# The low halves of one chunk's normalized rows, computed on DVE instead of POOL (attention, Fourier mixing and a feed-forward layer on one core)

## Chip, cores and metric

One core of a Trainium2 chip runs the whole kernel in one launch. The metric is the device time of that launch in microseconds (us), the median of several runs. The names of the engines are those of the profile: PE multiplies matrices (PEld is its weight load), DVE, ACT and POOL work elementwise, SP issues the DMAs.

## What is computed

```python
# q, k, v: (8, 8, 576, 64), phi: (8, 8, 576, 32), w_ch1: (512, 2048), w_ch2: (2048, 512), all f32
a = softmax(phi, axis=2)
k_m, v_m = a^T k, a^T v                        # 32 memories per head
attn = softmax(q k_m^T / 8) v_m                # per head
x = attn of all heads side by side             # (8, 576, 512)
u = x + real(fft(fft(x, axis=1), axis=2))
un = (u - mean(u)) / sqrt(var(u) + 1e-6)       # per row of 512
out = u + max(un @ w_ch1, 0) @ w_ch2
```

## The kernel before

The 4608 rows of the feed-forward layer form 36 tiles of 128 rows, and two tiles are a chunk: 18 chunks, numbered from 0. `background()` makes the tiles of `u` batch by batch (pooling, memories, scores, mixing); the feed-forward layer of one chunk runs while the background makes a later one.

**Chunk 0** is multiplied in f32 straight from the freshly decoded weights. The weights come in as 64-bit words, in 8 pieces j = 0..7 of `w1` and of `w2`. For each j the loop prepares a piece of `w1` (`prepare_w1`), multiplies (`ffn1_direct`, L701, PSUM tiles `ph_j_f`), prepares a piece of `w2` (`stage_w2`), multiplies again (`ffn2_direct`, L718, accumulating in `po_0` and `po_1`) and splits the piece of `w1` into f16 halves for the later chunks (`split_w1`). Preparing a piece is `to_f32`: ACT takes the high words (L797), DVE shifts them (L799) and joins sign and exponent (L800), and then the low words are folded in. For most pieces DVE folds (L810). For `w2` pieces 0, 2, 4 and 6 (the list `LP`) DVE shifts the low words (L805) and **POOL** adds them (L808). So PE's multiplication with `w2` piece 4 waits for POOL's L808 of that piece.

**Chunks 1 to 17** are multiplied in f16 pairs, high and low half. `norm_chunk(c)` makes them: the rows are normalized into `un` (POOL takes the root, L667; DVE scales, L668), ACT rounds both tiles to f16 into `ud[:, 0]` (L687), POOL subtracts, `ud[:, 1] = un - ud[:, 0]` (L688, 128 x 1024 elements), and SP issues one transposing DMA of `ud` into `unring` (L241). PE reads `unring` in `ffn1` (L258). Chunk 1 is normalized inside chunk 0's loop, as soon as four tiles of `u` exist.

The order on each engine is set ahead of time by a scheduler that simulates the program; within an engine, and in SP's queue of DMAs, instructions run strictly in that order. In SP's queue chunk 1's transposing DMA stands ahead of the weight loads (L787) of `w2` piece 6 and of both piece 7's.

```python
nc.gpsimd.tensor_tensor(out=d, in0=lo, in1=d, op=ALU.add)       # L808, pieces 2_0, 2_2, 2_4, 2_6
```

Of the kernel before, what the change touches and what calls it, by code (L numbers as in the profile page):

```python
# [16 lines left out]
ALU = mybir.AluOpType  # L17
# [114 lines left out]
def kernel(  # L132
# [10 lines left out]
    nc = tc.nc  # L143
# [21 lines left out]
    un = const.tile([P, CH, DM], F32, name="un")  # L165
    ud = const.tile([P, 2, CH, DM], F16, name="ud")
# [71 lines left out]
    def transpose(dst, src, on_pe, key):  # L238

        if not on_pe:  # L240
            nc.sync.dma_start_transpose(out=dst, in_=src)  # L241
            return
        n = src.shape[1] // P
        for i0 in range(0, n, 8):
            m = min(8, n - i0)
            pt = psg.tile([P, 512], F32, tag="g", name=f"pt_{key}_{i0}")
            ptv = pt.bitcast(F16)[:, : m * P]
            for i in range(m):
                nc.tensor.transpose(ptv[:, i * P : (i + 1) * P], src[:, (i0 + i) * P : (i0 + i + 1) * P], ident)
            nc.scalar.copy(out=dst[:, i0 : i0 + m], in_=ptv.rearrange("p (a c) -> p a c", c=P))  # L250
# [402 lines left out]
    def norm_tile(i, u, un):  # L653
        mv = tiny("mv", 2, 2)
        if i < 2 * BN:
            st = tiny("st", 6, 2)
            nc.vector.bn_stats(out=st, in_=u)
            nc.vector.bn_aggr(out=mv, in_=st)
        else:
            st = tiny("st", 6, 2)  # L660
            nc.scalar.activation(un, u, AF.Copy, scale=-1.0 / DM, accum_out=st[:, 0:1])
            nc.scalar.activation(un, u, AF.Square, bias=st[:, 0:1], accum_out=st[:, 1:2])
            nc.vector.tensor_scalar(out=mv[:, 0:1], in0=st[:, 0:1], scalar1=-1.0, scalar2=None, op0=ALU.mult)
            nc.vector.tensor_scalar(out=mv[:, 1:2], in0=st[:, 1:2], scalar1=1.0 / DM, scalar2=None, op0=ALU.mult)
        rs = tiny("rs", 1, 2)
        nc.vector.tensor_scalar(out=rs, in0=mv[:, 1:2], scalar1=1e-6, scalar2=0.25, op0=ALU.add, op1=ALU.mult)  # L666
        nc.gpsimd.tensor_tensor(out=rs, in0=rs, in1=half, op=ALU.pow)  # L667
        marks[f"un{i}"] = nc.vector.tensor_scalar(  # L668
            out=un, in0=u, scalar1=mv[:, 0:1], scalar2=rs, op0=ALU.subtract, op1=ALU.mult
        )  # L670

    def norm_chunk(c):

        unT = unring[:, c % 2]
        unT0 = unT.rearrange("p l t k c -> p (l t k c)").bitcast(F32)
        unT0 = unT0.rearrange("p (k t c) -> p k t c", k=NK, t=CH)
        for i in range(CH):
            idx = CH * c + i
            norm_tile(idx, us[idx], un[:, i])
            if c == 0:  # L680
                pt = psg.tile([P, 512], F32, tag="g", name=f"pt_unT_{i}")
                for k in range(NK):
                    nc.tensor.transpose(pt[:, k * P : (k + 1) * P], un[:, i, k * P : (k + 1) * P], identf)
                marks["uh0"] = nc.scalar.copy(out=unT0[:, :, i], in_=pt.rearrange("p (k c) -> p k c", k=NK))  # L684
        if c == 0:
            return unT0
        marks[f"uh{c}"] = nc.scalar.copy(out=ud[:, 0], in_=un)  # L687
        marks[f"ul{c}"] = nc.gpsimd.tensor_tensor(out=ud[:, 1], in0=un, in1=ud[:, 0], op=ALU.subtract)  # L688
        transpose(
            unT.rearrange("p l t k c -> p (l t k) c"), ud.rearrange("p l t c -> p (l t c)"), False, f"unT_{c}"  # L690
        )
        return unT
# [181 lines left out]
    marks = {}  # L874
# [100 lines left out]
    while made < 2:  # L975
        made, room = next(bg)
    unTs = {0: norm_chunk(0)}
    hs = {c: [] for c in range(n_chunks)}
    po = [ps2.tile([P, 512], F32, tag="o", name=f"po_0_{t}") for t in range(CH)]
    for j in range(NW):  # L980
        if j not in parts_w1:
            load_weights(j)
        after(GATE1[j], prepare_w1, j)
        ffn1_direct(j)
        after(GATE2[j], stage_w2, j)
        ffn2_direct(j, po)
        split_w1(j)
        advance(0, steps=STEPS)
        if made >= 2 * CH and 1 not in unTs:
            unTs[1] = norm_chunk(1)  # L990
# [15 lines left out]
    run_ffn1(NW + 4)  # L1006
    advance(CH, CH * 3)
    unTs[2] = norm_chunk(2)
    for n in range(NW, n_steps):
        c, j = divmod(n, NW)  # L1010
# [75 lines left out]
```

## Time and profile before

| | |
|---|---|
| time, median of 3 runs (lowest, highest) | 1002.51 us (1002.23, 1004.06) |
| span of the profiled execution | 1006.9 us |
| PE busy in it | 959.2 us (95%) |
| DVE, ACT, POOL busy | 567.1, 454.0, 233.0 us |
| L688 on POOL: 17 instructions | 45.1 us in all |

The span is the time from the first to the last instruction of one profiled execution. No other time of that execution is given. It is 4.4 us (0.4%) above the median of the unprofiled runs, so a sum worked out in the span is carried over to the median as a difference. Rows give times in us from the start of the span.

### The profile page before, as it was taken

The page shows a single profiled execution, that of the slowest core. Times are in us where ns is not written, and L with a number is a line of the kernel's source. Part 1 is how long each engine was busy: PE and PEld are TensorE (multiplying, and loading weights), DVE is VectorE, ACT ScalarE, POOL GpSimd, SP SyncE. Part 2 cuts the span into 40 slices and gives each one's busy share as a digit, 9 for nine tenths or more (in the row PEclk, how much of TensorE's full clock was granted, in tenths as well). Part 3 has the DMA queues.
Part 4 walks back from the last instruction along what each step waited for, and adds up shares of the span by engine and source line. Part 5 has one row for each costly group of instructions (what it writes and reads, how often), then busy time and mean ns, then how long its engine had stood idle before and what let it go on. Part 6 is the DMA issues. An engine that isn't in the chain of part 4 may idle for free.

```text
span 1006.9 us, 18664 instructions
## 1 busy us (share of the span) xinstructions
PE 959.2 (95%) x7644; PEld 685.4 (68%) x7644; DVE 567.1 (56%) x1300; ACT 454.0 (45%) x910; POOL 233.0 (23%) x249
## 2 busy tenths in 40 slices
PE   6769799789999999999999999999999999999998
PEld 6756478556677767777767767776777767666664
DVE  3789677767645575657542477557744675311111
ACT  2365347676534553655341555465545543311110
POOL 1212525234221231233120033113311322200000
PEclk9979899899999999999999999999999999999999
DMA  9706455053321622273210542254214310201000
GB/s 352 261 1 251 147 178 158 12 126 104 74 49 29 157 84 53 44 163 91 68 22 21 116 119 59 49 116 119 66 43 83 78 25 28 43 21 42 1 21 22
DMA packets 115958, 88.07 MB, mean 87 GB/s; under 512 B 100384, under 2 KB 100384, under 8 KB 113824
## 3 DMA queue, kind: packets, MB, share of 16 engines
q1 hardware_dynamic: 115872, 86.87, 32.3%
q8 instruction: 60, 0.98, 0.4%
q14 instruction: 26, 0.21, 0.1%
HBM read 58.15 MB, written 9.44 MB: 67 GB/s over the span
## 4 chain that ended last, share of the span: by engine, by line
PE 82%; DVE 9%; ACT 3%; issue 3%; POOL 1%; DMA 1%; SPq 0%; DVEq 0%; ACTq 0%; POOLq 0%
PE po L754 33%; PE ph L258 33%; PE pm L258 5%; PE pp_t L258 3%; PE psc L258 2%; PE po L718 2%; PE px_t L258 1%; PE pa L574 1%; PE ph L701 1%; PE pv L547 1%; DVE uring L643 1%; DVE un L668 1%; DMA rawt<-in_raw 1%; PE pf L324 1%; DVE w1t L810 1%
## 5 line engine op out<-in xcount | busy, mean ns | idle before, releaser
L258 PE MATMUL ph<-unring,w1t 128*128 128x256 f16 x3264 | 390.2, 273 | 0.4 <-DVE hring L745 0.4
L754 PE MATMUL po<-w2s,hring 128*128 128x512 f16 x1632 | 381.0, 381 | 6.7 <-ACT w2s L864 4.0
L258 PEld LDWEIGHTS <-w1t 128*128 128x128 f16 x3264 | 315.7, 98 | 65.0 <-issue 2.4
L754 PEld LDWEIGHTS <-hring 128*128 128x128 f16 x1632 | 158.2, 99 | 167.1 <-issue 10.0
L745 DVE SCALAR_TENSOR_TENSOR hring<-ph,hring 128x512 f16<-128x512 f32 x136 | 93.3, 686 | 168.3 <-ACT hring L744 167.7
L744 ACT ACTIVATE hring<-ph 128x512 f16<-128x512 f32 x136 | 80.1, 589 | 174.6 <-PE ph L258 174.3
L667 POOL TENSOR_TENSOR scratch<-scratch,small 128x1 f32<-128x1 f32 x36 | 24.3, 691 | 165.6 <-DVE scratch L666 153.6
L482 POOL TENSOR_TENSOR aring<-aring,scratch 128x384 f32<-128x384 f32 x28 | 24.3, 868 | 164.7 <-DVE scratch L480 152.0
L688 POOL TENSOR_TENSOR ud<-un,ud 128x1024 f16<-128x1024 f32 x17 | 45.1, 2650 | 47.6 <-ACT ud L687 47.6
L258 PEld LDWEIGHTS <-stg 128*128 128x128 f16 x1152 | 45.8, 98 | 9.6 <-issue 2.5
L399 POOL TENSOR_TENSOR stg<-rawt,stg 128x640 f16<-128x640 f32 x12 | 17.7, 1472 | 134.5 <-ACT rawt L398 114.3
L718 PE MATMUL po<-w2s,hring 128*128 128x512 f32 x64 | 32.5, 637 | 9.4 <-POOL w2s L808 6.5
L258 PE MATMUL pm<-et,stg 128*128 128x64 f16 (+1 forms) x780 | 38.9, 203 | 1.4 <-DMA et<-elt 0.9
L466 DVE TENSOR_REDUCE scratch<-psc 128x12 f32<-128x384 f32 x32 | 17.8, 555 | 37.3 <-PE psc L258 37.1
L629 DVE SCALAR_TENSOR_TENSOR share<-pp_t,scratch,small 128x257 f32<-128x257 f32 (+1 forms) x48 | 21.1, 480 | 29.4 <-ACT small L626 29.3
L258 PE MATMUL pp_t<-vh,at 128*128 128x255 f16 (+3 forms) x288 | 36.7, 273 | 0.9 <-ACT at L589 0.9
L501 ACT CAST aeo<-eo 128x384 f16<-128x384 f32 x30 | 15.3, 510 | 43.8 <-DVE eo L498 43.7
L643 DVE SCALAR_TENSOR_TENSOR uring<-px_t,scratch,share 128x256 f32<-128x256 f32 (+1 forms) x80 | 33.8, 476 | 0.2
L701 PE MATMUL ph<-unring,w1t 128*128 128x256 f32 x128 | 32.5, 401 | 0.5 <-ACT unring L684 0.5
L687 ACT CAST ud<-un 128x1024 f16<-128x1024 f32 x17 | 17.8, 1045 | 32.8 <-DVE un L668 24.6
L490 POOL TENSOR_TENSOR ahring<-aring,ahring 128x320 f16<-128x320 f32 x29 | 23.9, 825 | 36.7 <-ACT ahring L489 36.6
L258 PEld LDWEIGHTS <-at 128*128 128x128 f16 (+1 forms) x288 | 28.4, 102 | 5.6 <-issue 1.6
(238 smaller groups left out, 1258.6 us busy)
## 6 DMA issues: line engine op xcount, KB each, us to landing
rawt<-in_raw SPq DMA_DIRECT2D x15, 640.0 KB, 5.2
stg<-in_raw SPq DMA_DIRECT2D x15, 640.0 KB, 4.4
out<-uring SPq DMA_DIRECT2D x36, 256.0 KB, 2.1
stg<-in_w SPq DMA_DIRECT2D x7, 1024.0 KB, 5.9
rawt<-in_raw SPq DMA_DIRECT2D x15, 384.0 KB, 3.1
stg<-in_raw SPq DMA_DIRECT2D x15, 384.0 KB, 3.3
phs<-in_raw SPq DMA_DIRECT2D x32, 160.0 KB, 3.8
w2s<-in_w SPq DMA_DIRECT2D x4, 1024.0 KB, 9.6
```

The lines of the kernel that those rows point to most:

```text
L258: m = nc.tensor.matmul(out, lhsT=lhsT, rhs=rhs, start=start, stop=stop)
L482: eng.tensor_tensor(out=a, in0=a, in1=sm.unsqueeze(2).to_broadcast([P, 12, M]), op=ALU.mult)
L490: nc.gpsimd.tensor_tensor(out=ahl[:, :, 64:128], in0=av[:, 0:5], in1=ahl[:, :, 0:64], op=ALU.subtract)
L629: nc.vector.scalar_tensor_tensor(out=tm[rows, w * NJ : (w + 1) * NJ], in0=pp[rows, :NJ], scalar=beta[rows], in1=qs[rows], op0=ALU.mult, op ...
L643: nc.vector.scalar_tensor_tensor(out=u[rows, hs], in0=px[rows, hs], scalar=igx[rows], in1=tm[rows, w * NJ + half : w * NJ + half + 256], o ...
L667: nc.gpsimd.tensor_tensor(out=rs, in0=rs, in1=half, op=ALU.pow)
L688: marks[f"ul{c}"] = nc.gpsimd.tensor_tensor(out=ud[:, 1], in0=un, in1=ud[:, 0], op=ALU.subtract)
L701: nc.tensor.matmul(ph, lhsT=w[:, k, f * P : (f + 1) * P], rhs=unTs[0][:, k], start=(k == 0), stop=(k == NK - 1))
L718: nc.tensor.matmul(po[t], lhsT=h[:, f, t], rhs=w[:, f], start=(j == 0 and f == 0), stop=(j == NW - 1 and f == UB - 1),)
L744: nc.scalar.activation(h[:, 0], phv, AF.Relu)
L745: nc.vector.scalar_tensor_tensor(out=h[:, 1], in0=phv, scalar=0.0, in1=h[:, 0], op0=ALU.max, op1=ALU.subtract)
L754: nc.tensor.matmul(po[t], lhsT=hs[j][:, lh, f * 2 + t], rhs=w2s[:, j * UB + f, lw, :], start=(j == 0 and f == 0 and i == 0), stop=(j == NW ...
```

## The change

For chunk 1 alone the subtraction of L688 goes to DVE. The operands, the values and everything for the other 16 chunks are as before; chunk 0 has no such subtraction.

```diff
         marks[f"uh{c}"] = nc.scalar.copy(out=ud[:, 0], in_=un)
-        marks[f"ul{c}"] = nc.gpsimd.tensor_tensor(out=ud[:, 1], in0=un, in1=ud[:, 0], op=ALU.subtract)
+        eng = nc.vector if c == 1 else nc.gpsimd
+        marks[f"ul{c}"] = eng.tensor_tensor(out=ud[:, 1], in0=un, in1=ud[:, 0], op=ALU.subtract)
```

Lines behind it move down by one: L689 is the subtraction in the changed kernel, L702, L719, L800, L801, L806, L809, L811 and L835 are L701, L718, L799, L800, L805, L808, L810 and L834 of before.

On POOL the only difference is that the first L688 is gone: L808 of `w2` piece 4, which stood right behind it, now stands right behind chunk 1's two roots (L667). In SP's queue the transposing DMA and the weight loads behind it keep their places.

On DVE, in chunk 0's loop where pieces 4 and 5 are decoded, before:

```order
L800 SCALAR_TENSOR_TENSOR w2s<-w2s 128x1024
L834 SCALAR_TENSOR_TENSOR w1t<-w1t,small 128x1024
L810 SCALAR_TENSOR_TENSOR w1t<-stg,w1t 128x1024
L800 SCALAR_TENSOR_TENSOR w2s<-hring,w2s 128x512
L800 SCALAR_TENSOR_TENSOR w2s<-uring,w2s 128x512
```

and with the change:

```order
L801 SCALAR_TENSOR_TENSOR w2s<-w2s 128x1024
L835 SCALAR_TENSOR_TENSOR w1t<-w1t,small 128x1024
L689 TENSOR_TENSOR ud<-un,ud 128x1024
L811 SCALAR_TENSOR_TENSOR w1t<-stg,w1t 128x1024
L801 SCALAR_TENSOR_TENSOR w2s<-hring,w2s 128x512
L801 SCALAR_TENSOR_TENSOR w2s<-uring,w2s 128x512
```

The subtraction stands two behind the L800 that ends DVE's part of `w2` piece 4, and ahead of the fold of `w1` piece 5 (`w1t<-stg`).

On DVE some ten instructions later, at the end of that stretch, before:

```order
L800 SCALAR_TENSOR_TENSOR w1t<-stg,w1t 128x1024
L304 RECIPROCAL scratch<-scratch 128x1
L805 TENSOR_SCALAR stg<-stg 128x1024
L300 TENSOR_SCALAR scratch<-scratch 128x1
L810 SCALAR_TENSOR_TENSOR w1t<-stg,w1t 128x1024
L305 TENSOR_SCALAR phs<-phs,scratch 128x576
```

and with the change:

```order
L801 SCALAR_TENSOR_TENSOR w1t<-stg,w1t 128x1024
L304 RECIPROCAL scratch<-scratch 128x1
L300 TENSOR_SCALAR scratch<-scratch 128x1
L811 SCALAR_TENSOR_TENSOR w1t<-stg,w1t 128x1024
L305 TENSOR_SCALAR phs<-phs,scratch 128x576
L303 TENSOR_SCALAR scratch<-scratch 128x1
L806 TENSOR_SCALAR stg<-stg 128x1024
```

L805 (L806), which waits for the DMA of `w2` piece 6, now stands behind four more instructions, among them the fold of `w1` piece 6 (L810, L811).

On PE, where the products with `w2` piece 4 begin, before:

```order
L701 MATMUL ph_4_1_892<-unring,w1t 128x256 x4
L701 MATMUL ph_5_0_969<-unring,w1t 128x256 x4
L718 MATMUL po_0_492<-w2s,hring 128x512
L718 MATMUL po_1_493<-w2s,hring 128x512
L718 MATMUL po_0_492<-w2s,hring 128x512
L718 MATMUL po_1_493<-w2s,hring 128x512
L701 MATMUL ph_5_1_975<-unring,w1t 128x256 x4
```

and with the change:

```order
L702 MATMUL ph_4_1_892<-unring,w1t 128x256 x4
L719 MATMUL po_0_492<-w2s,hring 128x512
L719 MATMUL po_1_493<-w2s,hring 128x512
L702 MATMUL ph_5_0_969<-unring,w1t 128x256 x4
L719 MATMUL po_0_492<-w2s,hring 128x512
L719 MATMUL po_1_493<-w2s,hring 128x512
L702 MATMUL ph_5_1_975<-unring,w1t 128x256 x4
```

The group `ph_5_0` (8 instructions in the trace, two to each row here) has moved behind the first pair of products that need POOL's L808.

## Rows read from the trace of the kernel before

**Rows 1.** The page's head, PE's busy time, and PE and its granted clock in 40 equal slices.
```profile
span 1006.9 us, 18664 instructions
PE 959.2 (95%) x7644; PEld 685.4 (68%) x7644; DVE 567.1 (56%) x1300; ACT 454.0 (45%) x910; POOL 233.0 (23%) x249
...
PE   6769799789999999999999999999999999999998
...
PEclk9979899899999999999999999999999999999999
```

**Rows 2.** The longest wait of PE: who waited for whom, us in total, times, longest.
```profile
PE po L718 <- POOL w2s L808: 6.5, 1, 6.5
```

**Rows 3.** The chain of waits in order of time: start, us, what.
```profile
104.02 2.11 POOL ud L688
...
114.94 2.40 POOL w2s L808
...
117.38 5.73 PE po L718 x8
...
154.90 5.57 DMA rawt<-in_raw
```

**Rows 4.** All 17 instructions of L688: ns min/median/max, first and last start in us.
```profile
L688 POOL TENSOR_TENSOR ud<-un,ud x17: 2123/2129/10962, 104.0 to 873.1; 128x1024 f16<-128x1024 f32 x17
```

**Rows 5.** POOL in order of time: start, us, instruction, idle time before it.
```profile
69.13 2.73 POOL L808 TENSOR_TENSOR w2s<-w2s 128x1024 int32<-128x1024 int32 x1 [5.81 <-issue]
...
104.02 10.96 POOL L688 TENSOR_TENSOR ud<-un,ud 128x1024 f16<-128x1024 f32 x1 [5.29 <-ACT ud L687]
114.94 2.39 POOL L808 TENSOR_TENSOR w2s<-w2s 128x1024 int32<-128x1024 int32 x1
128.89 2.73 POOL L808 TENSOR_TENSOR w2s<-stg,w2s 128x1024 int32<-128x1024 int32 x1 [11.56 <-PE pl L311]
```

**Rows 6.** DVE in order of time, the same columns.
```profile
69.52 2.91 DVE L799 TENSOR_SCALAR w2s<-w2s 128x1024 int32<-128x1024 int32 x1
...
103.61 0.74 DVE L799 TENSOR_SCALAR w2s<-w2s 128x512 int32<-128x512 int32 x2
104.28 0.67 DVE L290 TENSOR_REDUCE scratch<-pf 128x1 f32<-128x512 f32 x1
104.88 1.20 DVE L800 SCALAR_TENSOR_TENSOR w2s<-w2s 128x1024 int32<-128x1024 int32 x1
106.02 1.27 DVE L834 SCALAR_TENSOR_TENSOR w1t<-w1t,small 128x1024 f16<-128x1024 f32 x1
107.21 1.21 DVE L810 SCALAR_TENSOR_TENSOR w1t<-stg,w1t 128x1024 uint32<-128x1024 uint32 x1
...
109.81 0.67 DVE L799 TENSOR_SCALAR w1t<-w1t 128x1024 int32<-128x1024 int32 x1
...
111.79 1.20 DVE L800 SCALAR_TENSOR_TENSOR w1t<-stg,w1t 128x1024 int32<-128x1024 int32 x1
112.92 0.14 DVE L304 RECIPROCAL scratch<-scratch 128x1 f32<-128x1 f32 x1
122.93 0.69 DVE L805 TENSOR_SCALAR stg<-stg 128x1024 uint32<-128x1024 uint32 x1 [9.86 <-DMA stg<-in_w]
...
129.28 2.67 DVE L305 TENSOR_SCALAR phs<-phs,scratch 128x576 f32<-128x576 f32 x1
...
132.47 0.68 DVE L810 SCALAR_TENSOR_TENSOR w1t<-hring,w1t 128x512 uint32<-128x512 uint32 x1
```

**Rows 7.** PE in order of time, the same columns.
```profile
103.83 1.89 PE L701 MATMUL ph<-unring,w1t 128*128 128x256 f32 x8
105.56 1.88 PE L718 MATMUL po<-w2s,hring 128*128 128x512 f32 x4
107.28 3.62 PE L701 MATMUL ph<-unring,w1t 128*128 128x256 f32 x16
117.38 5.73 PE L718 MATMUL po<-w2s,hring 128*128 128x512 f32 x8 [6.49 <-POOL w2s L808]
122.95 1.89 PE L701 MATMUL ph<-unring,w1t 128*128 128x256 f32 x8
...
134.38 0.60 PE L701 MATMUL ph<-unring,w1t 128*128 128x256 f32 x2
```

**Rows 8.** Stretches of the span: us, busy time of PE, PEld, DVE, ACT, POOL (instructions), PE's granted clock, share of the DMA engines, GB/s.
```profile
110.90:114.20 3.30, 0.00 (x0) 0.00 (x0) 2.17 (x6) 1.46 (x5) 3.30 (x1) 1.00 0.00 0
...
117.30:121.60 4.30, 4.22 (x5) 1.85 (x6) 0.00 (x0) 0.00 (x0) 0.03 (x1) 0.51 1.02 288
...
124.00:135.00 11.00, 10.98 (x44) 6.93 (x43) 10.27 (x16) 4.03 (x9) 2.73 (x1) 1.00 0.48 157
135.00:150.00 15.00, 14.99 (x87) 11.67 (x88) 8.29 (x26) 9.02 (x15) 3.83 (x4) 1.00 0.67 212
150.00:175.00 25.00, 24.97 (x229) 22.33 (x228) 19.65 (x65) 17.11 (x35) 13.41 (x18) 1.00 0.57 153
```

**Rows 9.** SP's queue in order of time: start, us, DMA.
```profile
115.01 1.86 SPq L241 DMA_TRANSPOSE unring<-ud  x1
116.98 1.08 SPq L787 DMA_DIRECT2D stg<-in_w  x1
```

**Rows 10.** ACT's last instruction before DVE's second L300 (the wait of which it releases).
```profile
112.71 0.20 ACT L297 ACTIVATION_READ_ACCUMULATOR phs<-pl,scratch 128x1 f32 x1
```

## The prediction, made before the changed kernel ran

> **What bounds the kernel now.** I read the page's head first. PE is busy for 95% of the span, and its granted clock dips only in the slices where PE has been idle [rows 1]: time can come only from PE's idle stretches and from the low clock behind them. The list of PE's waits comes next. Its longest single wait is 6.5 us, and it is for POOL's L808, the last step of `w2` piece 4 [rows 2]. The chain of waits says what made L808 late: L688 of chunk 1, behind which L808 is queued on POOL, and then PE's products [rows 3]. The reader is to see in the group of L688 that one of its 17 instructions took 10.96 us where the median is 2.13 us [rows 4].
>
> The timelines of POOL and DVE side by side show why. L688 starts at 104.02 and ends at 114.98 [rows 5]. In all that time DVE has no gap, and its work is mostly instructions with two operands in SBUF; its last long one ends at 111.79 + 1.20 = 112.99 [rows 6]. Counted back by its undisturbed 2.13 us, L688 got going at 112.85, just as that one finished. So POOL did not run slowly: it was kept out, for 8.8 us, past a dozen changes from one DVE instruction to the next. PE ran out of work at about 110.9 and went on at 117.38 [rows 7], and its first products ran at a granted clock of 0.51, the lower of its two levels (1.2 GHz) [rows 8]. From there PE has no gap up to 175 us [rows 8].
>
> **The change part by part.** *L688 leaves POOL* (-10.96 us there). L808 becomes free to ask as soon as DVE's L800 of its piece is done, at 104.88 + 1.20 = 106.08 [rows 6], where it now starts at 114.94 [rows 5]. The question on which all hangs is when it gets in.
>
> *L689 joins DVE.* The trace has no such TENSOR_TENSOR. The nearest row is L834, with the same shape, the same types (f16 out of f32 and f16) and both operands in SBUF: 1.27 us, and 1.19 us from its start to the next start (107.21 - 106.02) [rows 6]. I take 1.19. The bounds are 0.67 us (L799, one operand, the same number of elements [rows 6]) and POOL's 2.13 us [rows 4]. All that stands behind it in DVE's unbroken stretch moves by that much: the long L800 ends at 114.18.
>
> *When POOL gets in.* L808 asks at 106.1, in the middle of the very stretch that kept L688 out: L834, now L689, L810, the L800s, L799, L810s, L800. From 106.02 on that row is the same as before but for L689, again two operands in SBUF. So I take it that L808 is kept out as L688 was, up to the same place, 112.85 + 1.19 = 114.04. There the row opens again: L300 waits for ACT's L297 (before, it ended at 112.71 + 0.20 = 112.91 [rows 10]; it hangs on the same DVE chain and moves by the same 1.19), and the fold of `w1` piece 6 behind it needs the L800 that has only just ended. L808 then runs its 2.39 us [rows 5] and ends at 116.43. PE follows 0.05 us later (117.38 after 114.94 + 2.39 = 117.33), at 116.48: **0.90 us earlier** than before.
>
> *PE's order.* Before, `ph_5_0` was done ahead of the wait: 8 instructions, 1.73 us (105.56 - 103.83) [rows 7]. Now PE stops behind `ph_4_1`, at 107.28 + 1.73 = 109.01, and `ph_5_0` comes after: **1.73 us later** for all that follows. The break-even is an L808 that ends at 117.33 - 1.73 = 115.60.
>
> *Low clock.* PE idles about 7.4 us where it idled 6.49. Before, the 8 products after the wait took 122.95 - 117.38 = 5.57 us against 2 x (107.28 - 105.56) = 3.44 at full clock [rows 7]: 2.13 us. I take the same cost again, difference 0. Bounds: no fall at all (-2.13), or all of these products and `ph_5_0` at half speed (3.44 + 1.73 = 5.17, so +3.0).
>
> *The transposing DMA and the loads.* The DMA hangs on DVE's L689, which ends near 108.45, instead of 114.98, so it is issued 6.5 us earlier than at 115.01 [rows 9], and the weight load behind it (1.97 us later [rows 9]) at about 110.4 instead of 116.98. DVE's L805 was released by that load at 122.93, after 9.86 us of idle time [rows 6]; now it can be fed at about 116.4. I cost this at nothing: PE has no gap from 117.38 to 175 [rows 8], so nothing that arrives earlier there shortens it. That cover is gone only if PE comes some 5 us earlier (first rival). The L808 of piece 6 asks some 7 us earlier than its 128.89 [rows 5] while PE needs it later than 130, so it may be kept out for some 9 us without cost.
>
> Sum: -0.90 + 1.73 + 0 = **+0.8 us**. The sum is made against the span of 1006.9; on the median of 1002.51 it gives **1003.3 us**. Nothing behind it takes it back or adds to it: PE is gapless for 58 us, and the loads for the next batch follow PE (the DMA at 154.90 in the chain [rows 3]). Less than 2 us (0.2%) can't be told from no change in a measurement of this kernel.
>
> **A rule against the trace.** L688 waited through a dozen DVE instructions [rows 5, 6]. The Trainium skill ("SBUF — State Buffer", "Who interferes with whom") says that GpSimd and a DVE instruction with two SBUF inputs exclude each other, and that whichever issues first has the ports "for the whole instruction", while the other waits until it finishes. The trace agrees with the exclusion and not with a wait of one instruction. By that rule L808 would be held by L834 alone; the first rival works that out.
>
> **The rivals.** *POOL gets in at once* (faster). In two other places it did: L808 asked at 69.13 and 128.89 while a DVE instruction ran, took 2.73 us, 0.34 more than 2.39, and the next DVE instruction waited for it (L799 2.91 us, L305 2.67 us) [rows 5, 6]. Then L808 runs behind L834, from about 107.15 to 109.55; PE waits 0.5 us instead of 6.49 and the clock stays up. Against before, PE wins 6.49 + 2.13 - 0.5 = 8.1 us at that point. DVE, 2.05 us later for it, gives some back: `ph_5_0` needs the fold at 107.21, now done at 107.21 + 1.19 + 2.05 + 1.21 = 111.66, 0.4 us after PE asks; and `ph_7_0` (134.38 before [rows 7]) needs the fold of 132.47 [rows 6]. That one follows the load of `w2` piece 6, which lands about 4.3 us earlier, so 133.15 becomes about 128.8 at worst, while PE asks at about 124.9: up to 3.9 us, less if POOL's second L808 stays out of the way. Left: 8.1 - 0.4 - (1.3 to 3.9) = 3.8 to 6.4; I take 5: **997.5 us**. For it speak those two places; against it the 8.8 us of L688 in the same row of DVE's instructions.
>
> *POOL is kept out one place longer* (slower). The place is the change from the L800 that ends at 114.18 to the fold of `w1` piece 6. Before, L805 stood there and waited for its DMA, so DVE stopped and let POOL in [rows 6]; now the order puts work there that is ready. If the fold and L305 go first, L808 starts 1.2 to 1.9 us later and ends at 117.6 to 118.3: PE comes 2.0 to 2.7 us later than before, **1004.9 us**. It decides from an L808 that ends after 117.6. Against it: the fold needs the L800's result and can't be ready at its end.
>
> **How the numbers follow.** Forecast 0.55, POOL at once 0.28, POOL longer out 0.15, anything else 0.02. The forecast alone, with the clock's bounds, spans 1001.2 to 1006.3. The range leaves out its far end and part of the first rival: 997.0 to 1005.3. Faster by over 0.2%: 0.26 of the first rival and 0.03 of the forecast (no fall of the clock), 0.29. Slower by over 0.2%: 0.11 of the second rival and 0.05 of the forecast, 0.16. The rest, 0.55, is within 0.2%.
>
> **What would show it.** In the new profile L689 takes about 1.27 us on DVE; L808 of piece 4 starts near 106.1, takes about 10 us and ends near 116.4; PE waits about 7.4 us for it, from 109.1, and its clock falls once there; the transposing DMA is issued near 108.5; L806 starts before 119; PE then has no gap up to 175. An L808 of under 4 us with no fall of the clock near 110 means the first rival; one that ends after 117.6, the second. I am wrong altogether if PE's wait there goes and the time stays, or if the time moves by more than 2 us while these rows come out as said.

## The result: 6.6 us slower, and the profile after

| | before | changed |
|---|---|---|
| median time | 1002.51 us (five executions, 997.57 to 1004.06) | 1009.1 us (five executions, 1008.79 to 1011.29) |
| ratio | | 1.0075, interval 1.0054 to 1.0097 |
| span of the profiled execution | 1006.9 us | 1007.3 us |

The two lines of this table contradict each other: the medians are 6.6 us apart, the two profiled spans 0.4 us. The changed kernel's profiled execution is one of the five, and each of the five took 1.8 us more than its span (1009.1 with 1007.3). By the same 1.8 us the profiled execution of before took some 1008.7 us (an estimate), and that is 6 us more than its median. The medians alone give a ratio of 1.0066, inside the interval. In the later runs a single execution now and then took 1255 to 5455 us (2001 us for before); these are left out of every ratio.

First the profile after, beside what was foretold of it. The page's head, and PE's longest wait (who for whom, us in total, times, longest):

```profile
span 1007.3 us, 18664 instructions
```

```profile
PE po L719 <- POOL w2s L809: 7.2, 1, 7.2
```

The chain of waits of the changed kernel (start, us, what):

```profile
106.38 10.09 POOL w2s L809
116.51 3.78 PE po L719 x4
```

POOL, DVE, PE and SP in order of time (start, us, instruction, idle time before it):

```profile
106.38 10.08 POOL L809 TENSOR_TENSOR w2s<-w2s 128x1024 int32<-128x1024 int32 x1 [7.54 <-issue]
129.03 4.61 POOL L809 TENSOR_TENSOR w2s<-stg,w2s 128x1024 int32<-128x1024 int32 x1 [12.57 <-DVE w2s L801]
```

```profile
106.09 1.27 DVE L835 SCALAR_TENSOR_TENSOR w1t<-w1t,small 128x1024 f16<-128x1024 f32 x1
107.29 1.21 DVE L689 TENSOR_TENSOR ud<-un,ud 128x1024 f16<-128x1024 f32 x1
108.42 1.21 DVE L811 SCALAR_TENSOR_TENSOR w1t<-stg,w1t 128x1024 uint32<-128x1024 uint32 x1
...
113.01 1.20 DVE L801 SCALAR_TENSOR_TENSOR w1t<-stg,w1t 128x1024 int32<-128x1024 int32 x1
114.14 0.14 DVE L304 RECIPROCAL scratch<-scratch 128x1 f32<-128x1 f32 x1
124.23 0.21 DVE L300 TENSOR_SCALAR scratch<-scratch 128x1 f32<-128x1 f32 x1 [9.95 <-ACT phs L297]
...
125.98 0.69 DVE L806 TENSOR_SCALAR stg<-stg 128x1024 uint32<-128x1024 uint32 x1
```

```profile
107.38 1.89 PE L702 MATMUL ph<-unring,w1t 128*128 128x256 f32 x8
116.51 3.78 PE L719 MATMUL po<-w2s,hring 128*128 128x512 f32 x4 [7.25 <-POOL w2s L809]
120.09 2.66 PE L702 MATMUL ph<-unring,w1t 128*128 128x256 f32 x8
```

```profile
108.52 1.87 SPq L241 DMA_TRANSPOSE unring<-ud  x1
```

Against [rows 5 to 7, 9] the reader sees nearly what was foretold: L809 asks at 106.38, is kept out for 7.7 us through DVE's gapless row, and ends at 116.46 (foretold 116.43). PE waits 7.25 us and goes on at 116.51 (116.48). The transposing DMA is issued at 108.52 (108.5). Trace against trace, the step from before to after is +0.4 us, where +0.8 was worked out. So the place was read rightly, and yet the time is off by six: the error must lie in what it was compared with.

### The profile page after: what moved, and what is told of

It reads as the page before. It is cut to its first block, busy times and chain, and to the rows that moved or that the text cites. A ratio compares the mean times of both kernels' runs of the same rounds, so it can differ in the third digit from the quotient of the medians.

```text
span 1007.3 us, 18664 instructions
## 1 busy us (share of the span) xinstructions
PE 959.0 (95%) x7644; PEld 686.1 (68%) x7644; DVE 568.3 (56%) x1301; ACT 453.9 (45%) x910; POOL 231.1 (23%) x248
## 4 chain that ended last, share of the span: by engine, by line
PE 82%; DVE 9%; ACT 3%; issue 2%; POOL 2%; DMA 1%; SPq 0%; DVEq 0%; POOLq 0%; ACTq 0%
PE po L755 33%; PE ph L258 33%; PE pm L258 5%; PE pp_t L258 3%; PE psc L258 2%; PE po L719 2%; PE px_t L258 1%; PE ph L702 1%; POOL w2s L809 1%; PE pa L574 1%; PE pv L547 1%; DVE uring L643 1%; DVE un L668 1%; PE pf L324 1%; DMA rawt<-in_raw 1%
## 5 line engine op out<-in xcount | busy, mean ns | idle before, releaser
L667 POOL TENSOR_TENSOR scratch<-scratch,small 128x1 f32<-128x1 f32 x36 | 24.0, 681 | 165.6 <-DVE scratch L666 153.6
L689 POOL TENSOR_TENSOR ud<-un,ud 128x1024 f16<-128x1024 f32 x16 | 34.1, 2131 | 42.5 <-ACT ud L687 42.5
L719 PE MATMUL po<-w2s,hring 128*128 128x512 f32 x64 | 32.4, 633 | 10.1 <-POOL w2s L809 7.2
L702 PE MATMUL ph<-unring,w1t 128*128 128x256 f32 x128 | 33.4, 408 | 0.5 <-ACT unring L684 0.5
L702 PEld LDWEIGHTS ph<-unring,w1t 128*128 128x128 f32 x128 | 26.1, 208 | 9.1 <-issue 4.9
```

The lines of the kernel that those rows point to most:

```text
L689: marks[f"ul{c}"] = eng.tensor_tensor(out=ud[:, 1], in0=un, in1=ud[:, 0], op=ALU.subtract)
L702: nc.tensor.matmul(ph, lhsT=w[:, k, f * P : (f + 1) * P], rhs=unTs[0][:, k], start=(k == 0), stop=(k == NK - 1))
L719: nc.tensor.matmul(po[t], lhsT=h[:, f, t], rhs=w[:, f], start=(j == 0 and f == 0), stop=(j == NW - 1 and f == UB - 1),)
```

## The experiments

### Before, profiled again

The same kernel, unchanged: 12 executions, one of them profiled, and later one more with its own profile.

> The kernel before, unchanged. Its profiled execution had a span of 1006.9 us, but its median time is 1002.5, and the changed kernel's five executions lie 1.8 us above their own spans; so the profiled execution would itself have taken some 1008.7 us, 6 us above the median. Theory 1 (POOL's luck): in the usual executions of before POOL's first L688 is let in early and takes 2 to 4 us instead of 10.96, L808 of piece 4 then ends before PE asks for it or soon after, and PE's wait of 6.5 us and the low clock behind it (2.1 us) are mostly gone; an execution with a span of 1000 to 1001 us shows L688 under 5 us, one with a span of 1007 shows it near 11. Theory 2 (elsewhere): an execution with a span of 1000 to 1001 us shows the same L688 of 11 us and the same wait of PE, and is shorter in another place. Median time 1002.5 by both.

> The kernel before once more, one look for a further profile. Theory 1: the first L688 and PE's wait for L808 go with the span (short span: L688 under 5 us and PE's wait under 2 us; long span: 11 and 6.5 us). Theory 2: they do not.

Measured: 1003.31 us median (1001.88 to 1004.57), and 1004.12 us. With the medians of this and the other sets of before timed beside these experiments (1003.31 to 1004.33) for 1002.51, the loss of 6.6 us is rather 4.8 to 5.8. The two new profiles have spans of 1000.9 and 1002.3 us. In the first, all instructions of L688 (ns min/median/max), then POOL, DVE and PE:

```profile
L688 POOL TENSOR_TENSOR ud<-un,ud x17: 2123/2126/2300, 104.3 to 867.2; 128x1024 f16<-128x1024 f32 x17
```

```profile
104.34 2.30 POOL L688 TENSOR_TENSOR ud<-un,ud 128x1024 f16<-128x1024 f32 x1 [5.28 <-ACT ud L687]
107.86 3.32 POOL L808 TENSOR_TENSOR w2s<-w2s 128x1024 int32<-128x1024 int32 x1 [1.21 <-DVE w2s L800]
```

```profile
105.18 2.54 DVE L800 SCALAR_TENSOR_TENSOR w2s<-w2s 128x1024 int32<-128x1024 int32 x1
107.65 1.27 DVE L834 SCALAR_TENSOR_TENSOR w1t<-w1t,small 128x1024 f16<-128x1024 f32 x1
108.84 3.42 DVE L810 SCALAR_TENSOR_TENSOR w1t<-stg,w1t 128x1024 uint32<-128x1024 uint32 x1
```

```profile
108.85 1.89 PE L701 MATMUL ph<-unring,w1t 128*128 128x256 f32 x8
112.36 1.97 PE L701 MATMUL ph<-unring,w1t 128*128 128x256 f32 x8 [1.62 <-issue]
114.17 3.60 PE L718 MATMUL po<-w2s,hring 128*128 128x512 f32 x8
```

Here the 10.96 us of [rows 4] are gone. L688 got in at once (2.30 us) and DVE's L800 waited for it instead (2.54 us, 1.20 in [rows 6]). L808 got in at the next change, and ended at 111.18, 6.15 us before the 117.33 of [rows 5]. PE paused for 1.62 us where it had waited 6.49, for DVE's fold L810, which POOL had held up; it resumed 0.10 us after it. The other profile has the same picture (L688 2.31 us, L808 3.32 us). Theory 1 holds for these three traces: the profile that the prediction was read from was one of before's rare long executions. Of the more than 80 timed beside these experiments, five lie above 1007 us (1007.16 to 1011.03); they left no traces, so that POOL was kept out in them too is not shown.

With that the 6.4 us between the spans 1000.9 and 1007.3 add up. PE's granted clock in stretches, before (short execution) and then changed (start:end, length, busy PE, PEld, DVE, ACT, POOL with instructions, PE's granted clock, DMA share, GB/s):

```profile
94.60:110.70 16.10, 16.10 (x52) 10.41 (x52) 16.10 (x28) 9.62 (x17) 9.40 (x4) 0.89 0.57 168
```

```profile
94.40:109.30 14.90, 14.70 (x52) 9.29 (x52) 14.90 (x29) 9.60 (x17) 7.18 (x3) 1.00 0.42 145
...
116.50:125.00 8.50, 8.49 (x20) 4.99 (x21) 0.77 (x2) 2.15 (x6) 0.00 (x0) 0.70 0.23 85
```

PE stands still 7.25 - 1.62 = 5.6 us longer. At the lower of its two levels it loses, in the changed kernel, (1 - 0.70) x 8.5 = 2.6 us behind the wait, and in before (1 - 0.89) x 16.1 = 1.8 us at an earlier place: 0.8 us more. 5.6 + 0.8 = 6.4. The 1.8 us at the earlier place are no effect of the change, which begins only behind it: a second profile of the changed kernel has the low clock there too (0.89 from 94.40 to 109.30), PE waits 5.99 us in it instead of 7.25, and its span is 1007.2 us.

### PE's wait for POOL taken away, in both kernels

```diff
-LP = ["2_0", "2_2", "2_4", "2_6"]
+LP = ["2_0", "2_2", "2_6"]
```

> Before, with the last step of w2 piece 4 (shift and add of the low words) folded by DVE, as for the odd pieces, so that PE does not wait for POOL there, whatever POOL's L688 of chunk 1 does. Theory 1: this path no longer has two outcomes; spans lie within 1.5 us of each other, and at or below the short ones of before (time 999 to 1003 us). Theory 2: the two lengths of before stay, 6 us apart, and the median moves by under 2 us.

> The changed kernel with the same edit: DVE folds w2 piece 4, so PE does not wait for POOL's add of that piece. Theory 1 (the changed kernel is slow because its add of piece 4 is kept out every time): the 6.6 us over before are gone, and its time is within 2 us of before with the same edit. Theory 2 (the loss lies elsewhere): it stays 5 to 7 us above before with the same edit.

> The changed kernel with w2 piece 4 folded by DVE once more, since the profile of the first time (span 982.5 us) is the shortest of its six executions (median time 990.5). A span of 987 to 993 us is expected; the rows from 15 to 40 us tell whether the short one gained its 7 us there, in PE's transposed products before the first chunk, and not by the edit.

Measured: before with the edit 998.0 us (994.07 to 999.31; ratio to before 0.9917, 0.989 to 0.9943); the changed kernel with it 990.54 us (984.26 to 994.59; 0.9849, 0.9817 to 0.9881), and 990.37 in a second profiled execution of it. Two expectations failed: the executions of before with the edit were to lie within 1.5 us of each other and lie 5.2 apart, and the two kernels were to end within 2 us of each other.

That the loss hangs on this wait is seen where PE reaches its first L309, 10 to 13 us behind the wait. Before (short execution) and the changed kernel, then the same two with the edit (for the changed kernel its second profile):

```profile
122.77 0.60 PE L309 MATMUL pt_e<-identf,phs 128*128 128x128 f32 x4
```

```profile
129.47 0.60 PE L309 MATMUL pt_e<-identf,phs 128*128 128x128 f32 x4
```

```profile
122.62 0.60 PE L309 MATMUL pt_e<-identf,phs 128*128 128x128 f32 x4
```

```profile
123.23 0.60 PE L309 MATMUL pt_e<-identf,phs 128*128 128x128 f32 x4
```

With PE's wait the changed kernel comes 6.7 us later, without it 0.6. That it ends 7.5 us *faster* was expected by neither theory, and it comes later: the order behind the edit differs between the two, and one stretch holds most of it (before with the edit, then the changed kernel with it, second profile):

```profile
170.00:230.00 60.00, 48.83 (x369) 32.52 (x367) 40.53 (x93) 39.65 (x73) 17.52 (x13) 0.91 0.28 60
```

```profile
170.00:230.00 60.00, 55.29 (x478) 39.11 (x475) 44.30 (x105) 46.21 (x84) 22.09 (x19) 1.00 0.33 77
```

PE is idle there for 11.2 us in the one and 4.7 in the other. How much of that is the subtraction and how much the new order was not separated. This version beats both kernels. Its execution of 984.26 us gained its 7 us ahead of all this, between 15 and 42 us, as the second profile (which lacks them) shows; the last section returns to it.

### Is it DVE's added instruction, or the moment at which POOL asks?

POOL keeps its L688, but with 16 columns for 1024; a `memset` at the start of the kernel, not printed here, leaves the other columns zero. DVE gets nothing.

```diff
-        marks[f"ul{c}"] = nc.gpsimd.tensor_tensor(out=ud[:, 1], in0=un, in1=ud[:, 0], op=ALU.subtract)
+        w = slice(0, 8) if c == 1 else slice(0, DM)
+        marks[f"ul{c}"] = nc.gpsimd.tensor_tensor(out=ud[:, 1, :, w], in0=un[:, :, w], in1=ud[:, 0, :, w], op=ALU.subtract)
```

> Before, with POOL's subtraction for chunk 1 cut to 8 columns of each of its two tiles (128x16 elements); the rest of those low halves stays zero, which leaves that part of the computation out. The order on every engine is that of before and DVE has no L689, so only the size of POOL's L688 changes: L808 of piece 4 asks about where the changed kernel's L809 asks (106.4 us), some 0.29 us into DVE's L834. Theory A (what keeps POOL out is the moment at which it asks): L808 is kept out here as in the changed kernel, takes 8 to 10 us, PE waits over 5 us for it, and the time is 1006 to 1010 us. Theory B (what keeps it out is DVE's added L689 in the row): L808 is let in when L834 ends, ends near 110, PE waits under 1 us, and the time is 999 to 1003 us, at or below the usual executions of before.

> The changed kernel once more, for a second profile. If its add of piece 4 is kept out in every execution, as its five times within 2.5 us of each other suggest: L809 asks near 106.4 and takes about 10 us again, span 1006.5 to 1010 us. If it is a matter of luck there too: an L809 of 3 to 5 us and a span near 1001.

Measured: 1006.09 us (1005.02 to 1008.52), ratio 1.0037 (1.0016 to 1.0059); POOL and PE in it:

```profile
103.89 0.40 POOL L689 TENSOR_TENSOR ud<-un,ud 128x16 f16<-128x16 f32 x1 [5.28 <-ACT ud L687]
106.08 9.03 POOL L809 TENSOR_TENSOR w2s<-w2s 128x1024 int32<-128x1024 int32 x1 [1.79 <-DVE w2s L801]
```

```profile
115.16 5.14 PE L719 MATMUL po<-w2s,hring 128*128 128x512 f32 x8 [4.39 <-POOL w2s L809]
```

L809 asks where the changed kernel's does and is kept out as there, with no L689 on DVE. So DVE's added instruction is not what keeps POOL out. Taking work *off* POOL was enough to make the kernel slower: in both short profiles of before the long L688 gets in, DVE gives way, and the L808 behind it then gets in too. But this kernel loses 2.7 us (1006.09 with 1003.36) and not 6.6, and PE waits 4.39 us in it, less than the 5 of theory A and the 7.25 of the changed kernel. The difference is the two smaller terms of the prediction: without L689 the add ends 1.35 us earlier (115.11 for 116.46), and `ph_5_0` is done ahead of the wait (1.73 us), as in before. So being kept out makes less than half of the loss, and the longer row and PE's new order, which matter only where PE waits, make most of the rest. A second profile of the changed kernel gave 1008.93 us and an L809 of 10.08 us, to the hundredth the same.

### The reverse: L688 of before asks later

One more ACT copy (128x128, then 128x512) that L688 has to wait for, writing the same values again.

```diff
         marks[f"uh{c}"] = nc.scalar.copy(out=ud[:, 0], in_=un)
+        if c == 1:
+            marks[f"uh{c}"] = nc.scalar.copy(out=ud[:, 0, 0, :128], in_=un[:, 0, :128])
```

> Before, with one more ACT copy of 128x128 behind L687 (it writes the same values once more), which POOL's L688 waits for: L688 asks some 0.3 us later, at about 104.4 to 104.6, inside DVE's L290 and not inside the L799 ahead of it. The order on DVE and PE is the same up to there. Theory A (time: the later POOL asks into DVE's gapless row, the surer it is kept out, and L688 of before asks at the edge): L688 is kept out to the end of the row in nearly every execution (10 us), and PE waits 6 us for L808. Theory B (what stands in the row: an L290 that reads PSUM lets POOL in): L688 gets in during L290 or at its end, takes 2.1 to 2.8 us, and PE waits under 2 us.

> The same with a copy of 128x512: L688 asks some 0.65 us later than in before, at about 104.7 to 105.0, at the end of L290 or in the L800 behind it, which like its successors works on SBUF alone. Theory A: kept out to the end of the row (9 to 10 us). Theory B: kept out too if it asks in L800, let in if it still asks in L290. If it gets in from within L800, neither holds and the place in the row does not decide.

Measured: 1006.81 us (ratio 1.0026, 1.0012 to 1.0039) and 1006.39 us (1.0026, 1.0004 to 1.0048). POOL in the one and in the other:

```profile
105.53 9.50 POOL L690 TENSOR_TENSOR ud<-un,ud 128x1024 f16<-128x1024 f32 x1 [6.71 <-ACT ud L689]
```

```profile
106.13 9.23 POOL L690 TENSOR_TENSOR ud<-un,ud 128x1024 f16<-128x1024 f32 x1 [7.01 <-ACT ud L689]
```

L688 (here L690) is kept out in both, and no execution of the first is under 1005.7 us: a later request turns before's good luck into the long outcome. PE's wait in the first:

```profile
118.42 5.19 PE L720 MATMUL po<-w2s,hring 128*128 128x512 f32 x8 [7.43 <-POOL w2s L810]
```

In the second PE has one more group ahead of the wait and waits 4.48 us. That the medians are only 2.9 and 2.5 us above before's (1003.87) is due to another order further on, which gives some 2 us back: PE reaches the L309 of above at 128.62 in the first, 5.9 us behind the short execution of before, and the span is only 3.9 us longer (1004.8 with 1000.9). The first copy came later than meant and missed L290 (it asks in the L800 behind it), so these two don't tell the time in the row from what stands in it; theories A and B both allow them.

### A tiny instruction in DVE's row

```diff
+        if c == 1:
+            with tc.issue_after(marks["uh1"].ins):
+                nc.vector.tensor_scalar(out=tiny("gap", 1, 1), in0=ud[:, 0, 0, 0:1], scalar1=2.0, scalar2=None, op0=ALU.mult)
         marks[f"ul{c}"] = eng.tensor_tensor(out=ud[:, 1], in0=un, in1=ud[:, 0], op=ALU.subtract)
```

> The changed kernel with one more DVE instruction: a multiplication of a single column (128x1), which stands between L835 and L689 in DVE's row. In the measurement of the dispute by itself, rows with such a tiny instruction let POOL in at it 32 times of 32. Theory A (what costs the 6.6 us is that L809 is kept out of DVE's gapless row): L809 asks near 106.3, gets in when L835 ends and ends near 109.8, PE waits under 1.5 us for it instead of 7.2, its clock does not fall there, and the time is 997 to 1003 us in spite of the added instruction. Theory B (the loss hangs on something else, such as PE's new order): L809 may get in early, but the time stays at 1007 to 1011 us. If the tiny instruction does not open the row, L809 takes 10 us as before, and the time is 1008 to 1011 us.

Measured: 1009.35 us (ratio to before 1.0045, 1.0023 to 1.0068). The third case of the expectation came: the instruction stands in its place (here L691), and L812 (L809 of the changed kernel) takes 10.14 us.

```profile
105.43 1.27 DVE L838 SCALAR_TENSOR_TENSOR w1t<-w1t,small 128x1024 f16<-128x1024 f32 x1
106.63 0.14 DVE L691 TENSOR_SCALAR scratch<-ud 128x1 f32<-128x1 f16 x1
106.69 1.21 DVE L692 TENSOR_TENSOR ud<-un,ud 128x1024 f16<-128x1024 f32 x1
```

```profile
105.73 10.14 POOL L812 TENSOR_TENSOR w2s<-w2s 128x1024 int32<-128x1024 int32 x1 [7.54 <-issue]
```

Two of its executions (1003.33 and 1002.09) were short; they left no trace. Their granted clock (0.979 and 0.980; 0.984 to 0.988 in the others) points to the early rise of the clock told of in the last section (0.988 in the short execution there, 0.991 to 0.993 in the others of its kernel), and not to POOL, but that is not shown.

### The dispute by itself

Three kernels with nothing but DVE rows, POOL adds and the ACT copies that set the moment at which POOL asks.

> Not the layer but a measurement of the dispute by itself (nothing of the reference is computed): 128 times, DVE runs a row of 8 to 16 instructions of 128x1024 without a gap, and POOL asks for an int32 add of 128x1024 (2.4 us alone) at a moment that an ACT copy of 32 to 1024 columns moves by about 30 ns from one time to the next. Four rows, 32 moments each: subtractions with two operands; shifts with one; both in turn; and two-operand subtractions with tiny 128x1 instructions between. Theory A (the moment decides): in one and the same row POOL is let in at the next change for most moments (it takes under 3.8 us) and kept out through several instructions for a band of them. Theory B (the kind of the instructions decides): all moments of one row come out alike, and rows differ. By the rule of the Trainium skill (the page SBUF — State Buffer, section Who interferes with whom) POOL never waits longer than the one instruction that runs, so no add takes over 2.4 + 1.3 = 3.7 us.

> A second measurement of the dispute by itself (nothing of the reference is computed), all with two-operand subtractions of 128x1024 on DVE and int32 adds of 128x1024 on POOL, five groups of 23 times. Groups 1 and 2: DVE stands still for about 1 us ahead of each row (it waits for ACT), and POOL asks early in the row (group 1) or some 5 us into it (group 2). Group 3: the same, and POOL asks twice in a row. Groups 4 and 5: no stop is forced, as in the first measurement, rows of 9 and of 14. Theory A (a row that begins behind a stop of DVE lets POOL in, a row that follows the last without a stop does not): groups 1 and 2 all in (under 3.8 us), in group 3 the first add in; groups 4 and 5 in turn in and out, since each add that is kept out makes DVE stop. Theory B (every second of POOL's requests loses, whatever DVE did): groups 1 and 2 in turn in and out, and in group 3 the first in and the second out every time.

> A third measurement of the dispute by itself (nothing of the reference is computed). Every time DVE stops first and then runs 13 to 27 instructions without a stop; POOL's first add of 128x1024 asks early and its second asks k = 0 to 7 microseconds after the first is done, each k at 6 moments. Three rows behind the first four: two-operand subtractions alone (tt); in turn with reductions of 512 columns of PSUM, as DVE's L290 in the kernel (red); in turn with a tiny 128x1 instruction (tiny). Theory A (DVE's long gapless row shuts POOL out, and what comes next in the row can open it): the first add is always let in; in tt the second is kept out to the end of the row from some k on (it takes 6 us or more); in red it is let in at the next change to a reduction (under 3.8 us) at every k, which would be why POOL's L688, behind which L290 stands, usually gets in, while the changed kernel's L809, behind which only SBUF work stands, does not. Theory B (what is next does not matter): red and tiny keep the second add out as tt does. Theory C (only some state of the start): no second add is kept out in any row.

First measurement, POOL, the row of two-operand subtractions:

```profile
11.53 3.00 POOL L63 TENSOR_TENSOR p<-p,p 128x1024 int32<-128x1024 int32 x1 [11.09 <-ACT p L60]
22.84 10.92 POOL L63 TENSOR_TENSOR p<-p,p 128x1024 int32<-128x1024 int32 x1 [8.31 <-ACT p L60]
34.33 2.95 POOL L63 TENSOR_TENSOR p<-p,p 128x1024 int32<-128x1024 int32 x1 [0.57 <-ACT p L60]
45.65 10.87 POOL L63 TENSOR_TENSOR p<-p,p 128x1024 int32<-128x1024 int32 x1 [8.37 <-ACT p L60]
```

In three of the four rows the adds were let in and kept out strictly in turn (48 of 96 each; 2.3 to 3.4 us, and 7.1 to 15.7), whatever the moment and the kind of instruction: neither theory. Those kept out had asked 4.58 us (in the mixed row) to 13.72 us after POOL's last add. An add that was kept out made DVE stop and wait for it, and the next was let in; an add that was let in left DVE running, and the next was kept out. In the row with tiny instructions all 32 got in; none of them asked later than 5.77 us after the last.

Second: all 138 adds got in (2.3 to 3.4 us), also those that asked 5 us behind the stop. Groups 4 and 5 had a short stop in every row after all (the first subtraction waited for the copy ahead of it), so they test nothing more.

Third, POOL at the seventh and eighth value of k in the row of subtractions alone:

```profile
971.97 2.41 POOL L70 TENSOR_TENSOR p<-r,p 128x1024 int32<-128x1024 int32 x1 [7.68 <-ACT r L69]
...
998.81 15.76 POOL L70 TENSOR_TENSOR p<-r,p 128x1024 int32<-128x1024 int32 x1 [7.96 <-ACT r L69]
```

The brackets tell how long ago POOL's last add was done. All 42 adds that asked up to 7.68 us after it got in; all 6 that asked 7.96 us or more after it were kept out until DVE's row ended. In the rows with reductions of PSUM or tiny instructions all 96 got in. What fits all three is that a DVE row shuts POOL out once it has run long enough on SBUF work without a stop and without giving way; how long is enough differs from row to row.

In the kernel the edge lies elsewhere but the direction is the same. At this place of DVE's row, the adds and subtractions of 128x1024 that asked 5.26 to 5.28 us after POOL's last turn got in (three profiles of before and of its first edit); the one of [rows 5] asked 5.29 us after it and was kept out; all that asked 6.71 to 7.54 us after it were kept out (five profiles of four kernels). The time since the last turn does not decide alone: the L808 of [rows 5] at 128.89 asked 11.56 us after it, behind a stop of DVE (0.71 us at 127.20), and got in. The 9.03 us of L809 behind the subtraction with 16 columns (it asked 1.79 us after it) don't fit unless so short a turn, for which DVE did not give way, doesn't count.

## Why the prediction was wrong

**The step that failed** is the one that carried the sum from the profiled execution to the median. The prediction worked out +0.8 us against a span of 1006.9 and added it to 1002.51, as if the 4.4 us between them were a constant. They were not: a span can't be longer than the whole execution that it is part of, so a span above the median, and above all three times then known (1002.23 to 1004.06), says that this execution was none of the usual ones. Against that execution's own 1008.7 us the sum gives 1009.5; measured were 1009.1. Against the usual executions the change removes nothing (L688 takes 2.30 us there, not 10.96) and brings in the wait. The prediction's own last sign of being wrong came true: the time moved by more than 2 us while nearly all the rows came out as said.

**Step by step.** L689 on DVE: foretold 1.27 us and 1.19 to the next start, measured 1.21 and 1.13. POOL kept out up to DVE's last long L800 (L801 now): right, 116.46 for 116.43. By the rule of the Trainium skill that was weighed ("SBUF — State Buffer", "Who interferes with whom") POOL would have waited for one instruction; in these runs it waited through thirteen (10.08 us) and, in the measurement of the dispute, for 15.76 us. PE's order: right, it stops at 109.3 (109.01). The low clock at that place: foretold as unchanged, 2.13; by the stretch above it lost 2.6. So PE comes to its L309 1.35 us later than in the profile of before (129.47 with 128.12), of which some 0.9 are given back further on, where the prediction had nothing taken back. The earlier DMA and loads cost nothing: right, PE has no gap from 116.51 to 180.4. L806 before 119: wrong, 125.98. DVE's L300 stood 9.95 us for ACT's L297, because ACT's own queue stood behind PE's `ph_5_0`, which now comes after the wait for L809:

```profile
109.37 0.38 ACT L705 ACTIVATE hring<-ph 128x256 f32<-128x256 f32 x1 [1.25 <-PE ph L702]
122.84 0.38 ACT L705 ACTIVATE hring<-ph 128x256 f32<-128x256 f32 x1 [13.10 <-PE ph L702]
```

It cost nothing, and the L809 of piece 6 (4.61 us at 129.03) did not either.

**The rivals.** The first (POOL gets in at once, L808 behind L834, PE held up for 0.4 us by the fold) describes how *before* itself usually runs. The numbers that spoke for it, the two places where POOL got in, were weighed only for the changed kernel. Had they been turned on before's own L688, the 8.8 us in which it was kept out would have stood out as one of 17 instructions [rows 4] and been suspected of not being there every time. The second rival (L809 ends after 117.6) did not come.

**What is shown and what is open.** Shown: the two short executions of before and the long one differ in whether L688 and L808 get in; the changed kernel's add is kept out in both profiles; without PE's wait for that add the loss is gone up to PE's L309; asking later suffices to be kept out. Open: why the changed kernel without the wait is 7.5 us faster, what in the chip settles who gets in (near 5.28 us, executions of the same kernel fall on both sides), and why a tiny instruction opened the rows of the measurement and not the kernel's.

## What to carry to other kernels

Compare the span of a profile with the median before any sum is made against it: if the span is the longer, look first for a stall in it that happens once among many instructions of its group, and profile again. A POOL instruction that asks late into a long gapless DVE row on SBUF can wait to the end of that row, so what matters is when it asks and not only how long it is; taking work off POOL can make this worse (+2.7 us here). The remedy that held here was to let nothing on PE's path wait for POOL beside such a row.

## What was not expected of the hardware

DVE and POOL do not simply take turns. In the third measurement's row of subtractions POOL's add of 2.34 us was let in at the next change up to 7.68 us after its last turn and kept out for 15 us from 7.96 us on, with all 48 on their own side. In the second every row that began behind a stop of DVE let it in (138 of 138): 5.8 to 6.6 us into the row behind a stop of 1.17 us, and up to 1.2 us into it behind a stop of 0.1 us.

Matmuls came at half the rate in a stretch whose granted clock reads 1.00: from 15 to 20 us the profiled execution of 982.5 us did 48 matmuls and the second profile of the same kernel 25, with PE busy throughout:

```profile
15.00:20.00 5.00, 5.00 (x48) 5.00 (x46) 0.75 (x4) 0.00 (x0) 0.00 (x0) 1.00 1.04 417
```

```profile
15.00:20.00 5.00, 5.00 (x25) 5.00 (x25) 0.42 (x2) 0.00 (x0) 0.00 (x0) 1.00 1.04 416
```

The 1.00 is not a reading there. The first record of the clock, a rise to the upper level, lies at 14.4 us in the first trace and at 50.8 us in the second, and a stretch without a record counts as 1.00. In the second trace the same six products take 0.94 us ahead of that record and 0.55 us behind it:

```profile
48.16 0.94 PE L574 MATMUL pa<-ct,aeo 128*128 128x145 f16 x6
```

```profile
51.24 0.55 PE L574 MATMUL pa<-ct,aeo 128*128 128x145 f16 x6
```

So PE is best read as running at the lower of its two levels (1.2 GHz) up to 50.8 us in the one execution and up to 14.4 us in the other, and this is where the 7 us come from; in the long and the short profile of before the first record lies near 50 us too, so the first two slices of [rows 1] tell nothing of the clock. Why the rise came so early in one execution, with PE doing the same work up to there, is open.
